# Attention steps of three kinds, with part of the rounding and subtracting moved to GpSimd

## The chip, the cores and the metric

The kernel runs on one core of a Trainium2 chip. A core has TensorE (matrix products, called PE in the profile, with PEld for its weight loads), VectorE (DVE), ScalarE (ACT), GpSimd (POOL) and SyncE (SP, which here only issues DMAs). The metric is the device time of one execution in microseconds, lower is better.

## What is computed

An attention with queries averaged in pairs, followed by a feed-forward block with a squared relu. All arrays are float32.

```
batch, n_heads, seq, head_dim = 4, 8, 1152, 64
q_pool = q.reshape(B, H, S // 2, 2, D).mean(axis=3)
scores = (1 / sqrt(D)) * matmul(q_pool, k^T)
scores = scores - max(scores, axis=-1)
attn   = exp(scores) / (sum(exp(scores)) + 1e-9)
x      = matmul(attn, v), heads side by side: 2304 x 512
h = x @ w_in (512 x 2048); g = s * relu(h)**2 + b; out = g @ w_out (2048 x 512)
```

## The kernel before

**Two formats.** A float32 value is split in a rounded part in a short format of TensorE (names ending in `h` or `vv`) and the rest (`l`); a product of two split values is then three fast products. A product of whole float32 values needs no split but takes TensorE longer: the trace shows it as two matmuls.

**The loop.** 32 heads are taken in 16 pairs. A head has 9 steps, one for each 128 of its keys, so a pair has 18 steps, and n % 18 counts them here ("step 9" is the first step of a pair's second, odd head). Line 600 runs over all 288 steps. A step n issues, on TensorE and in an order written out by hand in `ORD` (line 31):

- the scores of step n (`score_step`, line 466: four matmuls at line 472 into a PSUM tile `s`, of which there are two);
- the value products of step n - 3 (`value_step`, line 491, with `LAG` = 3), into the accumulators `o0`, `o1` of the head, one for each half of the queries;
- one or two products for the maxima of a later pair (`max_unit`, line 426: a matmul at line 442 into `m`, and a maximum by VectorE at line 443).

**Two kinds of steps.** In a split step ScalarE takes the exponential twice, once rounded into `ph` (line 480) and once in place in PSUM (line 482); VectorE subtracts the two into `pl` (line 484); the value products are six matmuls (lines 507, 509, 511: `ph` with `vv`, `ph` with `vl`, `pl` with `vv`, for each half). In a whole step (`WHOLE`, line 33: 7 of 18) ScalarE takes one exponential into `pe` (line 475), and the value products are two float32 products (line 501), which need only `vf`, the values as loaded.

**Around the steps.** `PREP` (line 36) gives the step at which each part of the preparation of the pair after next is issued: `ka`, `kb`, `qt` are transposes by VectorE; `qs` adds the queries on GpSimd; `ha`, `hb`, `qh` round keys and queries on ScalarE (through `hi_of`, line 196); `qm`, `qz` lay out rounded queries on ScalarE; `kl`, `ql` take the rests on GpSimd; `l0`, `l1` (`lay`, line 384) each issue five DMAs on SP. Keys and queries of the pair after that are loaded by 4 and 8 DMAs on SP at step 17 (lines 338, 344). The values of the next head are loaded at step 3 of a head (line 349), rounded and split on GpSimd (`prep_v`, line 412: `vv` and `vl`) at steps 7 and 16 of a pair (`VS`). The maxima of a head are sent by ScalarE's DMA queue (lines 457, 458, tile `c`) at steps 2 and 12. When a head ends, `finish` (line 516) has ScalarE copy four pieces out of `o0` and `o1` (lines 527, 528).

Every engine and every DMA queue works through its instructions in the order of issue. From pair 9 on, weights are also converted, one piece in a pair, with four VectorE and three GpSimd instructions each. After the attention the feed-forward block runs in sweeps over the weights (`Moe`, line 218).

Of the kernel before, what the change touches and what calls it, by code (L numbers as in the profile page):

```python
# [29 lines left out]

ORD = ("svfvvvfvv",) * 8 + ("vvfvvvfvs",)
KB = 384
WHOLE = (1, 3, 6, 9, 11, 13, 16)

PP = (("ka", 0), ("kb", 0), ("ha", 0), ("hb", 1), ("qs", 1), ("qt", 1), ("qm", 2), ("qh", 2), ("qz", 2), ("kl", 2), ("ql", 3), ("l0", 7))
PREP = (("ka", 10), ("qs", 11), ("kb", 13), ("qt", 15), ("ha", 14), ("hb", 14), ("qm", 16), ("kl", 16), ("qh", 16), ("qz", 17), ("ql", 17), ("l0", 0), ("l1", 9))
LD = 1
VS = (7, 16)
XT = (1, 2, 3, 5, 8)
# [15 lines left out]
def attention_moe_kernel(ctx: ExitStack, tc: tile.TileContext, q, k, v, w_in, w_out, s_in, b_in, out):  # L55
# [140 lines left out]
    def hi_of(eng, out, in_):  # L196
        if eng is nc.scalar:
            nc.scalar.activation(out, in_, AF.Copy)  # L198
        else:
            eng.tensor_scalar(out=out, in0=in_, scalar1=1.0, scalar2=0.0, op0=ALU.mult, op1=ALU.add)  # L200
# [150 lines left out]
    def prep_pair(p):  # L351

        kr, qr = kraw.pop(p), qraw.pop(p)
        kT = ap.tile([P, S], F32, tag="kT", bufs=2, name=f"kT{p}")
        qT = ap.tile([P, SQ], F32, tag="qT", bufs=2, name=f"qT{p}")
        qs = ap.tile([P, NBQ, 32], F32, tag="qs", name=f"qs{p}")
        kh = ap.tile([P, S], F32R, tag="kh", bufs=2, name=f"kh{p}")
        qh = ap.tile([P, SQ], F32R, tag="qh", bufs=2, name=f"qh{p}")
        krv = kr.rearrange("p j i -> p (j i)")
        lo, hi = slice(0, SQ), slice(SQ, S)  # L360

        def corner():
            assert holds.get("qm", -1) == p - 1
            for h in range(2):
                d = slice(h * D, (h + 1) * D)
                hi_of(nc.scalar, qm[d, d], qT[d, NT4 * P:])
            holds["qm"] = p

        def k_hi(part, last):
            hi_of(nc.scalar, kh[:, part], kT[:, part])  # L370
            if last:
                khs[p] = kh

        def q_hi():
            hi_of(nc.scalar, qh, qT)
            qhs[p] = qh

        def q_blocks():

            for h in range(2):  # L380
                r = slice(h * D, (h + 1) * D)
                hi_of(nc.scalar, qzs[p % 2][r, h].rearrange("p (t m) -> p t m", t=NT4), qT[r, :NT4 * P].rearrange("p (m t) -> p t m", t=NT4))

        def lay(h):
            hd = 2 * p + h
            kk, qq = kks[hd % 3], qqs[hd % 3].rearrange("p i a n -> p i (a n)")
            r = slice(h * D, (h + 1) * D)
            ks = ((f32(kk[D:P, 0, :]), kT[r]), (f32(kk[0:D]), f32(kh[r]).unsqueeze(1).to_broadcast([D, 2, S])))
            for dst, src in ks[::-1] if hd == 0 else ks:
                nc.sync.dma_start(dst, src)  # L390
            nc.sync.dma_start(f32(qq[0:D, 0, :]), f32(qh[r]))
            nc.sync.dma_start(f32(qq[D:P, 0, :]), f32(qh[r]))
            nc.sync.dma_start(f32(qq[0:D, 1, :]), qT[r])
            holds["k", hd % 3] = hd

        return {
            "ka": lambda: nc.vector.transpose(out=kT[:, lo], in_=krv[:, lo]),
            "qs": lambda: (nc.vector if p < 2 else nc.gpsimd).tensor_tensor(out=qs, in0=qr[:, :, 0, :], in1=qr[:, :, 1, :], op=ALU.add),
            "kb": lambda: nc.vector.transpose(out=kT[:, hi], in_=krv[:, hi]),
            "ha": lambda: k_hi(lo, False),  # L400
            "qt": lambda: nc.vector.transpose(out=qT, in_=qs.rearrange("p j i -> p (j i)")),
            "hb": lambda: k_hi(hi, True),
            "qh": q_hi,
            "qz": q_blocks,
            "kl": lambda: (nc.vector if p == 0 else nc.gpsimd).tensor_tensor(out=kT, in0=kT, in1=f32(kh), op=ALU.subtract),
            "ql": lambda: nc.gpsimd.tensor_tensor(out=qT, in0=qT, in1=f32(qh), op=ALU.subtract),
            "qm": corner,
            "l0": lambda: lay(0),
            "l1": lambda: lay(1),
        }  # L410
# [52 lines left out]
    prob = {}  # L463
    fresh = []

    def score_step(hd, j, eng):
        assert holds["k", hd % 3] == holds["c", hd % 3] == hd
        kk, qq = kks[hd % 3], qqs[hd % 3]
        ps = ps_s.tile([P, 2, 512], F32, tag="s", name=f"s{hd}_{j}")
        for a in range(2):  # L470
            for i in range(2):
                nc.tensor.matmul(ps[:, a, :HALF], kk[:, i, j * P:(j + 1) * P], qq[:, i, a], start=(i == 0), stop=(i == 1))  # L472
        if eng is None:
            pe = late.tile([P, 2, HALF], F32, tag="pe", bufs=PE, name=f"pe{hd}_{j}")
            nc.scalar.activation(pe, ps[:, :, :HALF], AF.Exp, scale=SCALE)
            prob[hd, j] = pe, None
            return
        ph = late.tile([P, 2, HALF], F32R, tag="ph", bufs=PB, name=f"ph{hd}_{j}")
        pl = late.tile([P, 2, HALF], F32R, tag="pl", bufs=PB, name=f"pl{hd}_{j}")
        nc.scalar.activation(ph, ps[:, :, :HALF], AF.Exp, scale=SCALE)  # L480

        nc.scalar.activation(ps[:, :, :HALF], ps[:, :, :HALF], AF.Exp, scale=SCALE)  # L482
        prob[hd, j] = ph, pl
        fresh.append(lambda: eng.tensor_tensor(out=pl, in0=ps[:, :, :HALF], in1=f32(ph), op=ALU.subtract))  # L484

    acc = {}
    xu = {}
# [3 lines left out]
    def value_step(hd, j):  # L491
        assert holds["v", hd % 2] == hd
        vv, vl = vvs[hd % 2], vls[hd % 2]
        ph, pl = prob.pop((hd, j))
        if j == 0:
            acc[hd] = [ps_o.tile([P, 512], F32, tag=f"o{a}", name=f"o{hd}_{a}") for a in range(2)]
        first, last = j == 0, j == NJ - 1
        for a in range(2):
            o = acc[hd][a]
            if pl is None:  # L500
                nc.tensor.matmul(o[:, :HALF], vfs[hd % 2][:, j], ph[:, a], start=first, stop=last)  # L501
                if a == 1 and last:
                    finish(hd)
                for _ in range(3):
                    yield
                continue
            nc.tensor.matmul(o[:, :HALF], vv[:, j], ph[:, a], start=first, stop=False)  # L507
            yield
            nc.tensor.matmul(o[0:D, :HALF], vl[:, j], ph[:, a], start=False, stop=False)  # L509
            yield  # L510
            nc.tensor.matmul(o[:, :HALF], vv[:, j], pl[:, a], start=False, stop=last)  # L511
            if a == 1 and last:
                finish(hd)
            yield

    def finish(hd):
        o = acc.pop(hd)
        p, h = divmod(hd, 2)
        if h == 0:
            xu[p] = (  # L520
                ep.tile([P, 2, HALF], F32, tag="xu", name=f"xu{p}"),
                ep.tile([P, 2, HALF], F32, tag="l", name=f"l{p}"),
            )
        x, l = xu[p]
        r = slice(h * D, (h + 1) * D)
        for a in range(2):
            nc.scalar.activation(x[r, a], o[a][0:D, :HALF], AF.Copy)
            nc.scalar.activation(l[r, a], o[a][D:P, :HALF], AF.Copy, bias=EPS)

        def invert():  # L530
            lt = ep.tile([P, NBQ, 32], F32, tag="lt", name=f"lt{p}")
            nc.vector.transpose(out=lt, in_=l.rearrange("p a n -> p (a n)"))
            inv[p] = lt

        def reciprocal():
            lt = inv[p]
            rc = inv[p] = ep.tile([P, NBQ, 1], F32, tag="rc", name=f"rc{p}")
            nc.vector.reciprocal(rc, lt[:, :, 0:1])

        def spread():  # L540
            rc = inv[p]
            inv[p] = ep.tile([P, NBQ, 32], F32, tag="lt", name=f"rr{p}")
            nc.vector.transpose(out=inv[p], in_=rc.to_broadcast([P, NBQ, 32]))

        def scale():
            xo = xs[p] = ep.tile([P, SQ], F32, tag="xo", name=f"xo{p}")
            nc.gpsimd.tensor_tensor(out=xo, in0=x.rearrange("p a n -> p (a n)"), in1=inv.pop(p).rearrange("p j c -> p (j c)"), op=ALU.mult)

        def send():
            nc.sync.dma_start(xd[hd // H][(hd % H) // 2], xs.pop(p))  # L550

        if h == 1:
            for at, fn in zip(XT, (invert, reciprocal, spread, scale, send)):
                later(at, fn)
# [45 lines left out]
    for n in range(NS + LAG):  # L600
# [4 lines left out]
        units = iter(range((n + AHEAD) * NU // 18, (n + AHEAD + 1) * NU // 18) if n + AHEAD < NS else ())  # L605
        for part in ORD[at] if at is not None else "sff":
            if part == "s" and n < NS:
                score_step(hd, j, None if n % 18 in WHOLE else nc.vector)
            elif part == "f":
                for u in units:  # L610
                    max_unit(u, ps_m, "m")
# [112 lines left out]
```

## Time and profile before

| | us |
|---|---|
| median of 3 runs (lowest to highest) | 1018.68 (1016.87 to 1018.93) |
| the profiled execution, its own time | 1018.46 |
| its span in the profile | 1016.6 |
| busy: PE, PEld | 927.6, 818.0 |
| busy: DVE, ACT, POOL | 651.7, 686.6, 379.6 |

The span is cut by eye into the start (to about 35 us), the attention (to 572 us) and the feed-forward block. A matmul's time in the profile runs from its start to a modelled end, and successive matmuls overlap; what one costs is read from start to start. In the lists, "[1.01 <-DVE pm L443]" is idle time of the engine just before an instruction, and what ended it. Line numbers are those of the kernel before.

### The profile page before, as it was taken

What the parts mean: (1) busy time and instruction counts of PE and PEld (TensorE: products, weight loads), DVE (VectorE), ACT (ScalarE), POOL (GpSimd) and SP (SyncE); (2) the same over time, 40 slices, a digit from 0 to 9 for tenths busy, and PEclk for the clock granted to TensorE, in tenths of its full rate; (3) what the DMA queues carried; (4) which work ended last, traced back from release to release, by engine and by line L of the source; (5) the groups of instructions that cost most, each with busy time, mean ns of one, the idle gap of its engine ahead of it and who ended that gap; (6) DMA issues with size and microseconds to landing.
All of it is one profiled execution on the core that took longest, in us unless ns stands there. A gap on an engine that the chain in (4) does not pass through costs nothing.

```text
span 1016.6 us, 16051 instructions
## 1 busy us (share of the span) xinstructions
PE 927.6 (91%) x5680; PEld 818.0 (80%) x5680; DVE 651.7 (64%) x1191; ACT 686.6 (68%) x1278; POOL 379.6 (37%) x270
## 2 busy tenths in 40 slices
PE   4899999999999999989989987888889999999998
PEld 2778888888788878878878876767779999999997
DVE  5677777777778777877876378777783333333333
ACT  2577677767776787778777777876666555555553
POOL 5323223423342335235523288786772010011000
PEclk9999999999999999999999999999999999999999
DMA  8769765876587669766762245554442313213211
GB/s 166 137 117 190 152 124 108 179 158 126 114 165 161 122 136 184 167 125 136 175 154 55 74 148 186 185 187 145 141 149 84 125 63 114 73 63 92 96 43 42
DMA packets 255311, 131.15 MB, mean 129 GB/s; under 512 B 203776, under 2 KB 227328, under 8 KB 255232
## 3 DMA queue, kind: packets, MB, share of 16 engines
q1 hardware_dynamic: 248064, 130.06, 53.5%
q10 hardware_dynamic: 7168, 0.08, 0.4%
q8 instruction: 45, 0.74, 0.3%
q14 instruction: 34, 0.28, 0.1%
HBM read 68.68 MB, written 18.87 MB: 86 GB/s over the span
## 4 chain that ended last, share of the span: by engine, by line
PE 56%; DVE 20%; ACT 12%; issue 5%; DMA 2%; POOL 2%; ACTq 1%; SPq 0%; DVEq 0%; POOLq 0%
PE y L287 13%; PE h L258 12%; PE s L472 10%; PE o L501 7%; PE m L442 6%; DVE pl L484 4%; DVE pm L443 3%; PE o L511 3%; PE o L509 3%; ACT s L482 3%; ACT ph L480 3%; PE o L507 2%; DVE wAo L152 2%; DVE wAi L152 2%; DVE wabo L151 1%
## 5 line engine op out<-in xcount | busy, mean ns | idle before, releaser
L443 DVE TENSOR_REDUCE pm<-m 128x1 f32<-128x384 f32 x432 | 230.1, 548 | 51.1 <-PE m L442 44.0
L472 PE MATMUL s<-qq,kk 128*128 128x288 f32 x1152 | 208.0, 307 | 18.1 <-DVE pl L484 16.0
L258 PE MATMUL h<-x,wih 128*128 128x256 f32 x1152 | 213.3, 282 | 3.7 <-POOL x L239 3.7
L472 PEld LDWEIGHTS s<-qq,kk 128*128 128x128 f32 x1152 | 170.8, 190 | 40.9 <-DVE pl L484 16.6
L258 PEld LDWEIGHTS h<-x,wih 128*128 128x128 f32 x1152 | 186.9, 189 | 16.6 <-POOL x L239 5.5
L484 DVE TENSOR_TENSOR pl<-s,ph 128x576 fp32r<-128x576 f32 x176 | 132.5, 753 | 85.9 <-ACT s L482 85.8
L442 PE MATMUL m<-kh,qz 128*128 128x384 f32 x384 | 167.5, 446 | 21.5 <-DVE pm L443 21.0
L267 DVE SCALAR_TENSOR_TENSOR t<-h,r 128x256 f32<-128x256 f32 x144 | 60.7, 421 | 168.3 <-ACT r L277 168.3
L480 ACT ACTIVATE ph<-s 128x576 fp32r<-128x576 f32 x176 | 113.9, 647 | 79.6 <-PE s L472 78.6
L258 PE MATMUL h<-x,wil 128*128 128x256 f32 x576 | 162.2, 282 | 0.0
L239 POOL TENSOR_TENSOR x<-xr,x 128x1024 fp32r<-128x1024 f32 x27 | 66.0, 2444 | 229.6 <-ACT x L198 229.6
L501 PE MATMUL o<-pe,vf 128*128 128x288 f32 x448 | 144.7, 407 | 0.0
L287 PE MATMUL y<-woh,gl 128*128 128x512 f32 x288 | 115.7, 402 | 24.9 <-DVE gl L274 24.9
L270 ACT ACTIVATE gh<-t,sb 128x256 fp32r<-128x256 f32 x144 | 86.2, 598 | 65.9 <-DVE t L267 65.8
L482 ACT ACTIVATE s<-s 128x576 f32<-128x576 f32 x176 | 114.2, 649 | 0.0
L287 PE MATMUL y<-wol,gh 128*128 128x512 f32 x288 | 113.2, 393 | 0.0
L287 PE MATMUL y<-woh,gh 128*128 128x512 f32 x288 | 112.8, 392 | 0.0
L258 PEld LDWEIGHTS h<-x,wil 128*128 128x128 f32 x576 | 109.5, 190 | 0.0
L442 PEld LDWEIGHTS m<-kh,qz 128*128 128x128 f32 x384 | 74.7, 195 | 43.1 <-DVE pm L443 33.9
L507 PE MATMUL o<-ph,vv 128*128 128x288 f32 x352 | 107.4, 305 | 0.2 <-POOL vv L200 0.2
L509 PE MATMUL o<-ph,vl 128*64 128x288 f32 x352 | 104.5, 297 | 0.9 <-POOL vl L417 0.9
L511 PE MATMUL o<-pl,vv 128*128 128x288 f32 x352 | 103.6, 294 | 0.0
(73 smaller groups left out, 1481.9 us busy)
## 6 DMA issues: line engine op xcount, KB each, us to landing
kk<-kh SPq DMA_DIRECT2D x32, 576.0 KB, 5.7
kraw<-in_k_dram SPq DMA_DIRECT2D x64, 144.0 KB, 3.1
qraw<-in_q_dram SPq DMA_DIRECT2D x128, 72.0 KB, 2.5
vf<-in_v_dram SPq DMA_DIRECT2D x32, 288.0 KB, 4.4
kk<-kT SPq DMA_DIRECT2D x32, 288.0 KB, 3.3
qq<-qh SPq DMA_DIRECT2D x64, 144.0 KB, 5.6
xr<-xd SPq DMA_DIRECT2D x18, 512.0 KB, 4.0
wsti<-in_moe_w_in_dram SPq DMA_DIRECT2D x16, 512.0 KB, 4.8
```

What stands on the lines that cost most here:

```text
L258: nc.tensor.matmul(h[:, :TB], st[:, c, :], mv[:, c, :], start=(n == 0), stop=(n == 3 * NC - 1))
L287: nc.tensor.matmul(y[:, :DM], st[:, ts_], mv, start=(first and n == 0), stop=(last and n == 2))
L442: nc.tensor.matmul(ps[:, :KB], st, khs[p][:, e * KB:(e + 1) * KB], start=True, stop=True)
L443: nc.vector.tensor_reduce(out=pms[p][:, col, e:e + 1], in_=ps[:, :KB], axis=AX.X, op=ALU.max)
L472: nc.tensor.matmul(ps[:, a, :HALF], kk[:, i, j * P:(j + 1) * P], qq[:, i, a], start=(i == 0), stop=(i == 1))
L480: nc.scalar.activation(ph, ps[:, :, :HALF], AF.Exp, scale=SCALE)
L482: nc.scalar.activation(ps[:, :, :HALF], ps[:, :, :HALF], AF.Exp, scale=SCALE)
L484: fresh.append(lambda: eng.tensor_tensor(out=pl, in0=ps[:, :, :HALF], in1=f32(ph), op=ALU.subtract))
L501: nc.tensor.matmul(o[:, :HALF], vfs[hd % 2][:, j], ph[:, a], start=first, stop=last)
L507: nc.tensor.matmul(o[:, :HALF], vv[:, j], ph[:, a], start=first, stop=False)
L509: nc.tensor.matmul(o[0:D, :HALF], vl[:, j], ph[:, a], start=False, stop=False)
L511: nc.tensor.matmul(o[:, :HALF], vv[:, j], pl[:, a], start=False, stop=last)
```

## The change

- Steps get one of three kinds by their place among the 18 (`KIND`): 7 are `v`, split steps as before, subtracted by VectorE in PSUM (0, 2, 5, 8, 10, 12, 15); 5 are `g` (3, 6, 9, 13, 16), in which ScalarE writes the second exponential into an SBUF tile `pe` and GpSimd subtracts; 6 are `w`, whole (1, 4, 7, 11, 14, 17). Before there were 11, none and 7.
- From the third pair on, keys and queries are rounded by GpSimd and not by ScalarE.
- The two accumulators become one tile of two banks, and `finish` copies two pieces of double width in place of four.
- The parts of the preparation are issued at other steps: `kb` 13 to 12, `ha` 14 to 12, `hb` 14 to 13, `qt` 15 to 14, `kl` 16 to 14, `qm` 16 to 15, `qz` 17 to 16, `l0` 0 to 3; `ka`, `qs`, `qh`, `ql`, `l1` stay.

```diff
-WHOLE = (1, 3, 6, 9, 11, 13, 16)
+KIND = "vwvgwvgwvgvwvgwvgw"
-PREP = (("ka", 10), ("qs", 11), ("kb", 13), ("qt", 15), ("ha", 14), ("hb", 14), ("qm", 16), ("kl", 16), ("qh", 16), ("qz", 17), ("ql", 17), ("l0", 0), ("l1", 9))
+PREP = (("ka", 10), ("qs", 11), ("kb", 12), ("ha", 12), ("hb", 13), ("qt", 14), ("kl", 14), ("qm", 15), ("qh", 16), ("qz", 16), ("ql", 17), ("l0", 3), ("l1", 9))
...
         def k_hi(part, last):
-            hi_of(nc.scalar, kh[:, part], kT[:, part])
+            hi_of(nc.scalar if p < 2 else nc.gpsimd, kh[:, part], kT[:, part])
...
         def q_hi():
-            hi_of(nc.scalar, qh, qT)
+            hi_of(nc.scalar if p < 2 else nc.gpsimd, qh, qT)
...
-    def score_step(hd, j, eng):
+    def score_step(hd, j, kind):
...
-        if eng is None:
+        if kind != "v":
             pe = late.tile([P, 2, HALF], F32, tag="pe", bufs=PE, name=f"pe{hd}_{j}")
+        if kind == "w":
             nc.scalar.activation(pe, ps[:, :, :HALF], AF.Exp, scale=SCALE)
...
-        nc.scalar.activation(ps[:, :, :HALF], ps[:, :, :HALF], AF.Exp, scale=SCALE)
+        full = ps[:, :, :HALF] if kind == "v" else pe
+        nc.scalar.activation(full, ps[:, :, :HALF], AF.Exp, scale=SCALE)
         prob[hd, j] = ph, pl
-        fresh.append(lambda: eng.tensor_tensor(out=pl, in0=ps[:, :, :HALF], in1=f32(ph), op=ALU.subtract))
+        eng = nc.vector if kind == "v" else nc.gpsimd
+        fresh.append(lambda: eng.tensor_tensor(out=pl, in0=full, in1=f32(ph), op=ALU.subtract))
...
-            acc[hd] = [ps_o.tile([P, 512], F32, tag=f"o{a}", name=f"o{hd}_{a}") for a in range(2)]
+            acc[hd] = ps_o.tile([P, 2, 512], F32, tag="o", name=f"o{hd}")
...
-            o = acc[hd][a]
+            o = acc[hd][:, a]
...
-        for a in range(2):
-            nc.scalar.activation(x[r, a], o[a][0:D, :HALF], AF.Copy)
-            nc.scalar.activation(l[r, a], o[a][D:P, :HALF], AF.Copy, bias=EPS)
+        nc.scalar.activation(x[r], o[0:D, :, :HALF], AF.Copy)
+        nc.scalar.activation(l[r], o[D:P, :, :HALF], AF.Copy, bias=EPS)
...
-                score_step(hd, j, None if n % 18 in WHOLE else nc.vector)
+                score_step(hd, j, KIND[n % 18])
```

## Rows read from the trace of the kernel before

**Rows 1.** The page's first part: busy us, share of span, instructions.
```profile
PE 927.6 (91%) x5680; PEld 818.0 (80%) x5680; DVE 651.7 (64%) x1191; ACT 686.6 (68%) x1278; POOL 379.6 (37%) x270
```
**Rows 2.** Stretches: length, busy PE, PEld, DVE, ACT, POOL, granted clock, DMA.
```profile
273.44:290.09 16.65, 15.73 (x103) 14.41 (x101) 13.04 (x23) 10.78 (x20) 2.56 (x3) 1.00 0.82 170
290.09:307.06 16.97, 15.59 (x94) 13.44 (x94) 12.43 (x23) 14.06 (x26) 8.47 (x6) 1.00 0.61 115
...
478.04:513.26 35.22, 31.84 (x195) 27.74 (x194) 28.08 (x50) 26.42 (x48) 14.92 (x11) 1.00 0.74 162
```
**Rows 3.** Groups by line: busy us, mean ns, idle before and its releaser.
```profile
L484 DVE TENSOR_TENSOR pl<-s,ph 128x576 fp32r<-128x576 f32 x176 | 132.5, 753 | 85.9 <-ACT s L482 85.8
L482 ACT ACTIVATE s<-s 128x576 f32<-128x576 f32 x176 | 114.2, 649 | 0.0
...
L417 POOL TENSOR_TENSOR vl<-vf,vv 128x576 fp32r<-128x576 f32 x32 | 45.8, 1432 | 2.3
...
L198 ACT ACTIVATE qz<-qT 64x512 fp32r<-64x512 f32 x32 | 35.7, 1117 | 0.2
...
L527 ACT ACTIVATE xu<-o 64x288 f32<-64x288 f32 x64 | 25.8, 404 | 20.1 <-PE o L511 19.3
...
L200 POOL TENSOR_SCALAR vv<-vf 128x576 fp32r<-128x576 f32 x32 | 21.5, 673 | 96.7 <-DMA vf<-in_v_dram 51.0 <-PE m L442 16.7 <-PE o L511 14.8
...
L198 ACT ACTIVATE kh<-kT 128x576 fp32r<-128x576 f32 x32 | 20.3, 679 | 7.1 <-DVE kT L397 6.8
```
**Rows 4.** TensorE in order of time (start, us, line, matmul): a split and a whole step.
```profile
278.28 0.34 PE L442 MATMUL m<-kh,qz 128*128 128x384 f32 x1
278.45 0.30 PE L509 MATMUL o<-ph,vl 128*64 128x288 f32 x1
278.59 0.29 PE L511 MATMUL o<-pl,vv 128*128 128x288 f32 x1
...
284.81 0.65 PE L501 MATMUL o<-pe,vf 128*128 128x288 f32 x2
...
285.47 0.65 PE L501 MATMUL o<-pe,vf 128*128 128x288 f32 x2
```
**Rows 5.** TensorE in order of time: the two longest stops of a pair.
```profile
275.66 0.80 PE L472 MATMUL s<-qq,kk 128*128 128x288 f32 x4 [0.92 <-DVE pl L484]
...
305.77 0.44 PE L442 MATMUL m<-kh,qz 128*128 128x384 f32 x1 [1.01 <-DVE pm L443]
```
**Rows 6.** One pair's way from `c` to the odd head's first value product, by engine.
```profile
273.44 0.49 ACTq L457 DMA_DIRECT2D qq<-c  x1
...
282.56 0.57 SPq L349 DMA_DIRECT2D vf<-in_v_dram  x1
...
288.86 0.67 POOL L200 TENSOR_SCALAR vv<-vf 128x576 fp32r<-128x576 f32 x1 [7.59 <-PE o L511]
...
290.99 1.43 POOL L398 TENSOR_TENSOR qs<-qraw 128x576 f32<-128x576 f32 x1
...
289.66 0.65 PE L501 MATMUL o<-pe,vf 128*128 128x288 f32 x2
```
**Rows 7.** The same `c` and `vv` in the first and last of 12 pairs.
```profile
105.28 0.49 ACTq L457 DMA_DIRECT2D qq<-c  x1
...
120.34 0.68 POOL L200 TENSOR_SCALAR vv<-vf 128x576 fp32r<-128x576 f32 x1 [7.23 <-PE o L511]
...
478.04 0.49 ACTq L457 DMA_DIRECT2D qq<-c  x1
...
491.09 0.67 POOL L200 TENSOR_SCALAR vv<-vf 128x576 fp32r<-128x576 f32 x1 [5.24 <-PE m L442]
```
**Rows 8.** SP's own waits from 60 to 560 us: total, times, longest.
```profile
SPq L344 <- DMA qq<-c: 103.4, 14, 10.4
```
**Rows 9.** Line 151's durations (ns: min/median/max), 370 to 560 and 580 to 760 us.
```profile
L151 DVE TENSOR_SCALAR wabi<-whmi x3: 428/428/428, 385.3 to 524.1; 128x512 int32<-128x512 int32 x3
...
L151 DVE TENSOR_SCALAR wabi<-whmi x13: 426/1330/1341, 580.1 to 748.4; 128x512 int32<-128x512 int32 x13
```

## The prediction, made before the changed kernel ran

> **What bounds the kernel now.** I read the page's shares first, then stretches of the length of a pair, then TensorE in order of time, then what feeds it. TensorE is busy 91% of the span, its weight loads 80%, no other engine over 68% [rows 1], at a granted clock of 1.00 in every stretch that I read [rows 2]. Only the attention changes, so it is read by itself. A pair takes 33.62 us in the middle of it (the first two rows together) [rows 2]; of 12 pairs from 105.28 to 513.26 us the first eight take 33.6 to 33.8, the last four, with weights to convert, 34.2 to 35.2 (the longest stands in the group) [rows 2].
>
> Busy matmuls overlap, so I count from start to start. A fast product costs 0.13 to 0.14, a maximum's product 0.17 [rows 4]. A whole half-step starts 0.66 before the next, with one maximum's product in between: 0.49 [rows 4]. A pair then needs 18 x 4 x 0.1325 for scores (9.5), 27 x 0.17 for maxima (4.6), 11 x 6 x 0.1325 for split steps (8.7) and 7 x 0.97 for whole ones (6.8): 29.6 of 33.6 us. The other 4 us are the small change at switches and stops. The two longest have an idle time of 0.92, where the scores wait for VectorE's subtraction to give PSUM back, and 1.01, where a maximum's product waits for VectorE's reduction, which stands in VectorE's order behind a subtraction that waits for ScalarE [rows 5]. ScalarE is late there because it has just laid out queries (2 x 1.12) and rounded them [rows 3]. So TensorE bounds the pair, and behind it the order of ScalarE and VectorE: the place where this change works.
>
> **The chain beside it.** One thing runs beside the pairs and matters here. Each pair, SP stops in the loads of queries until the DMA that ScalarE sends for the maxima of the odd head has landed: 14 stops, 103.4 us [rows 8]. Only then come the remaining query loads, the five DMAs of `l0` and the load of the odd head's values, issued at 282.56 where `c` was sent at 273.44; `vv` starts on GpSimd at 288.86, and `vl` ends as the next instruction starts, 290.99 [rows 6]. From `c` to `vv` it is 15.06 in the first and 13.05 in the last of 12 pairs [rows 7], 14.07 on average, at most 15.42. Before, this had just room: the first value step of the odd head (step 9) is whole, needs `vf` alone and starts at 289.66 [rows 6].
>
> **The change, part by part, for one pair.**
>
> *Kinds of steps.* TensorE: one whole step (0.97) becomes a split one (6 x 0.1325 = 0.80), 0.17 saved, on its path. VectorE: 4 subtractions fewer, 4 x 0.75 = 3.0 [rows 3]. ScalarE: one exponential more, 0.65 [rows 3]. GpSimd: 5 subtractions of 128x576 float32; the trace has the operation at 1.43 (`vl`) [rows 3], both inputs in SBUF, so 7.2. The PSUM tile of a `g` step is free after ScalarE's second exponential, 0.75 before it would be with VectorE behind.
>
> *Rounding.* ScalarE loses three instructions of 0.68, 2.0; GpSimd does the same shape in 0.67 (`vv`) [rows 3], 2.0. GpSimd goes from 11.03 of 33.62 us (2.56 and 8.47) [rows 2] to about 20, and from 14.92 to about 24 of 35 with weights. It has room on average; what counts is its order.
>
> *The held subtraction.* Step 9 is now `g`. In GpSimd's order its subtraction stands behind `vv` and `vl` of the odd head (issued at step 7), which wait for the load. Its exponentials are there at about 286, but it starts when `vl` ends: 14.07 + 0.75 + 1.38 after `c`, and ends 1.42 later, 17.6 after `c`. The value products of step 9 need it as their third matmul, which stood at 290.09, 16.65 after `c`. So TensorE waits about 1 us there if nothing ahead of it gets faster, and more by whatever it gains ahead. Queued behind: `qs`, then roundings of keys, the subtraction of step 13 and `kl`; step 13's result is used three steps later, so 5.6 us of queue fit. This chain sets the first part of the pair. The keys are transposed one step earlier, so one query load more may have gone before SP stops: 0 to 0.5 off the chain; I take 0.3, thus 17.3.
>
> *The second part*, from 290.09 to the next `c` at 307.06, is 16.97 [rows 2]. The whole step that went lies here (values of steps 9 to 17 held four, now three): 0.17 off. Stops, summed from start to start, are about 2.2, of which 1.2 is the one at 305.77 [rows 5]. ScalarE has 2.0 less rounding, the layout of queries a step earlier, VectorE half its subtractions. The bounds for what goes are 0.3 (only the small ones) and 2.2 (all); nearest to the long one is ScalarE's work just ahead of it, which is what the change removes, so I take 1.5: 15.3. What is late next is the product itself. Pair: 17.3 + 15.3 = 32.6, 1.0 less.
>
> *The accumulators.* Four copies of 0.40 become two of double width, by the exponentials' rows 0.65 each: 0.3 less a head [rows 3]. But the copies now start when the second half is done, and the next head's first product waits for both: 0 to 0.5 late, twice a pair. At the odd head the held subtraction hides it, at the even head it falls in the first part, where TensorE will wait anyway. So nothing; with that cover gone 16 x 1.0 = 16 us.
>
> *The moved parts.* `l0` issues five DMAs on SP at step 3 and no longer at 0; they stay ahead of the load of values and behind the query loads, at whose stop they already wait until step 4. Nothing, and 0 to 0.5 a pair if SP's order of waits shifts. `kb`, `ha`, `hb`, `qt`, `kl` come earlier by one or two steps and are needed at step 3 of the next pair: nothing. `ql` ends GpSimd's list of the pair, by my count at about step 2, before SP's stop ends.
>
> *Weights.* VectorE's line 151 takes 428 ns in the attention and 1330 in the later stretch where GpSimd is busier [rows 9]. Four such instructions in six pieces, each 0.9 longer, would be 22 us of VectorE; in the attention it has slack, and three of the four come while GpSimd waits for the load. I take 1 us, between 0 and 22. The Trainium skill (SBUF — State Buffer, Who interferes with whom) says that VectorE in a two-port mode, or with two SBUF inputs, and GpSimd shut each other out for a whole instruction. By that rule more GpSimd work lengthens these, and leaves the subtraction from PSUM alone; the rows agree as far as they go.
>
> **The sum.** 12 pairs x 1.0 = 12. The last 1.75 pairs (from 513 to 572 us) have no loads and so no chain; there the stops count whole, 1.7 of 3.3 plus 0.17: 3.3. For the first two pairs I take nothing. Less 1 for the weights: 14.3. From the profiled execution's 1018.46 (span 1016.6 and 1.9 around it, 0.2 under the median): 1004.
>
> **Rivals.**
> - *TensorE alone sets the pair.* If the loads come early enough (SP no longer stops for `c`, or one step later in the order), the held subtraction is in time and the pair is 29.5 plus about 1.5, 31: 2.6 x 13.5 = 35 us less, 984. For it: idle SP time of 7 to 10 us a pair [rows 8]; against: nothing in the change takes that wait away.
> - *The held subtraction takes more than the stops give back: slower.* Same place. It decides when `c` to subtraction exceeds 33.62 - 15.3 = 18.3, 1.0 beyond my value; three of the 12 pairs have a `vv` that late (over 15 after `c`). With 18.3 and only 0.7 of the stops saved the pair is 34.4, 0.8 x 12 = 10 us longer, less 3 at the end: 1025. For it: the wait is new in every pair, and the stops' cause on ScalarE gets an exponential back; against: the long stop sits right behind the work that leaves ScalarE.
> - *VectorE shut out during the weights.* The 22 us in full undo the gain: 1025. Against: VectorE's slack.
> - *No change.* The two cancel, within 0.2% (2 us, about what a measurement of this kernel can tell from none): 1018.
>
> **How the numbers follow.** Forecast (993 to 1013) 0.50; TensorE alone (975 to 993) 0.15; subtraction wins 0.20; VectorE shut out 0.04; cancel 0.11. Faster 0.65, same 0.11, slower 0.24. The range runs from 983, half of the first rival, to 1025, the middle of the second.
>
> **What would show it.** Right: matmuls of line 511 with `pl` of step 9 idle 1 to 3 us each pair, released by GpSimd's subtraction; 17 to 18 us from `c` to the end of that subtraction; no stop over 0.5 before the next `c`; VectorE 3 us and ScalarE 2 us less a pair. Wrong: no such wait (then 984), or waits for GpSimd also at steps 13 and 16, or the stop at the end of the odd head still there (then 1018 or above).

## The result and the profile after

The change made the kernel slower: 1023.93 us (1022.44 to 1026.02, four runs) against 1018.47 (1016.87 to 1018.93), a ratio of 1.0058 with a 95% interval of 1.0036 to 1.0079. I had forecast 1004. The profiled execution took 1022.44, its span 1020.6, 4.0 over that of before.

The load did move. This is the page's first part of the kernel after, to be held against [rows 1]:

```profile
PE 919.3 (90%) x5712; PEld 819.4 (80%) x5712; DVE 618.8 (61%) x1127; ACT 663.6 (65%) x1188; POOL 519.9 (51%) x392
```

TensorE has 8 us less work, VectorE 33, ScalarE 23; GpSimd has 140 more. So the time has gone into waiting. The groups by line name the wait (busy us, mean ns, idle before and its releaser, as in [rows 3]):

```profile
L474 PE MATMUL s<-qq,kk 128*128 128x288 f32 x1152 | 213.2, 310 | 35.9 <-ACT pe L478 20.8 <-DVE pl L489 12.3 <-POOL vv L202 1.2
...
L489 POOL TENSOR_TENSOR pl<-pe,ph 128x576 fp32r<-128x576 f32 x80 | 114.3, 1428 | 159.5 <-ACT pe L486 159.5
...
L489 DVE TENSOR_TENSOR pl<-s,ph 128x576 fp32r<-128x576 f32 x112 | 84.4, 754 | 49.0 <-PE o L516 21.7 <-ACT s L486 20.9 <-PE s L474 3.7
...
L531 ACT ACTIVATE xu<-o 64x576 f32<-64x576 f32 x32 | 20.6, 644 | 41.5 <-PE o L506 22.9 <-PE o L516 16.3 <-POOL vl L419 1.2
```

The scores' matmuls (L474) sit idle 20.8 us for `pe` of L478, the single exponential of a *whole* step. Before, no such wait was among the long ones, as the same group shows there:

```profile
L472 PE MATMUL s<-qq,kk 128*128 128x288 f32 x1152 | 208.0, 307 | 18.1 <-DVE pl L484 16.0 <-POOL vv L200 1.3 <-DVE pm L443 0.2
```

In order of time, all engines, one steady pair (its odd head's `c` goes at 276.50):

```profile
291.38 0.68 POOL L202 TENSOR_SCALAR vv<-vf 128x576 fp32r<-128x576 f32 x1 [4.19 <-DMA vf<-in_v_dram]
...
291.74 0.70 PE L474 MATMUL s<-qq,kk 128*128 128x288 f32 x4
...
292.00 0.65 ACT L531 ACTIVATE xu<-o 64x576 f32<-64x576 f32 x1 [1.17 <-PE o L516]
292.66 0.65 ACT L532 ACTIVATE l<-o 64x576 f32<-64x576 f32 x1
293.33 0.65 ACT L478 ACTIVATE pe<-s 128x576 f32<-128x576 f32 x1
...
293.50 1.41 POOL L489 TENSOR_TENSOR pl<-pe,ph 128x576 fp32r<-128x576 f32 x1
...
294.03 0.80 PE L474 MATMUL s<-qq,kk 128*128 128x288 f32 x4 [1.59 <-ACT pe L478]
...
295.11 0.29 PE L516 MATMUL o<-pl,vv 128*128 128x288 f32 x1
```

Read it from the bottom. The scores of step 12 start at 294.03, after a stop of 1.59. They wait for `pe` of step 11, which ends at 293.98. That exponential stands in ScalarE's order behind the two copies of the even head's accumulator, and these wait for the last value product. TensorE's written order puts the scores of steps 11 (291.74) and 12 back to back at the change of heads, with nothing between. In the built program the two have the same PSUM tile: the pool gave step 12 not the tile of step 10 but that of step 11. The trace bears it out: the scores of step 12 wait for ScalarE's semaphore in 13 pairs, and all 13 have this stop; with the tile of step 10, a `v` step, they would wait for VectorE's. (Step 10 has the tile of step 9 in five pairs, without a stop over 0.28.) In the kernel before, neighbours share a tile too, at steps 2, 7, 10 and 17 (and 14 in one pair), but never at 3 or 12, where two scores stand back to back.

The stretches, odd `c` to odd `c`, with the steady pair cut where the values of step 9 take their `pl` (length, busy PE, PEld, DVE, ACT, POOL, granted clock, DMA), against [rows 2]:

```profile
276.50:295.11 18.61, 16.00 (x102) 14.38 (x101) 11.70 (x21) 12.08 (x21) 7.85 (x7) 1.00 0.83 172
295.11:309.87 14.76, 14.74 (x97) 13.48 (x95) 11.21 (x21) 11.12 (x19) 12.05 (x10) 1.00 0.57 107
...
70.04:109.38 39.34, 33.45 (x197) 30.17 (x195) 23.15 (x42) 23.19 (x39) 23.31 (x19) 0.91 0.80 151
...
480.49:515.22 34.73, 31.10 (x197) 27.87 (x195) 26.24 (x46) 24.73 (x42) 23.78 (x20) 1.00 0.72 152
515.22:549.75 34.53, 30.85 (x197) 27.89 (x195) 25.00 (x43) 23.13 (x39) 21.10 (x16) 1.00 0.44 106
```

From these points the 4.0 us, and the 18.3 by which the forecast missed, can be laid out (us; the last column is what the prediction's sum gave):

| stretch | before | after | difference | forecast |
|---|---|---|---|---|
| start, to the third odd `c` | 105.28 | 109.38 | +4.1 | 0 |
| eight pairs without weights | 269.25 | 267.21 | -2.0 | -8.0 |
| four pairs with weights | 138.73 | 138.63 | -0.1 | -3.0 |
| the rest of the span | 503.34 | 505.38 | +2.0 | -3.3 |

### The profile page after: what moved, and what is told of

Its sections match the earlier page's. It is cut to its first block, busy times and chain, and to the rows that moved or that the text cites. A ratio compares the mean times of both kernels' runs of the same rounds, so it can differ in the third digit from the quotient of the medians.

```text
span 1020.6 us, 16183 instructions
## 1 busy us (share of the span) xinstructions
PE 919.3 (90%) x5712; PEld 819.4 (80%) x5712; DVE 618.8 (61%) x1127; ACT 663.6 (65%) x1188; POOL 519.9 (51%) x392
## 4 chain that ended last, share of the span: by engine, by line
PE 66%; DVE 14%; ACT 7%; issue 4%; POOL 3%; DMA 2%; SPq 1%; DVEq 0%; ACTq 0%; POOLq 0%
PE s L474 13%; PE y L289 13%; PE h L260 12%; PE o L506 8%; PE m L444 7%; PE o L512 5%; PE o L516 4%; PE o L514 4%; DVE wAo L154 2%; DVE wAi L154 2%; DVE wabi L153 1%; DVE wabo L153 1%; DVE whmi L151 1%; DVE whmo L151 1%; ACT h L273 1%
## 5 line engine op out<-in xcount | busy, mean ns | idle before, releaser
L474 PE MATMUL s<-qq,kk 128*128 128x288 f32 x1152 | 213.2, 310 | 35.9 <-ACT pe L478 20.8
L474 PEld LDWEIGHTS s<-qq,kk 128*128 128x128 f32 x1152 | 172.9, 191 | 54.8 <-ACT pe L478 26.2
L489 POOL TENSOR_TENSOR pl<-pe,ph 128x576 fp32r<-128x576 f32 x80 | 114.3, 1428 | 159.5 <-ACT pe L486 159.5
L483 ACT ACTIVATE ph<-s 128x576 fp32r<-128x576 f32 x192 | 124.9, 651 | 106.4 <-PE s L474 80.4
L444 PE MATMUL m<-kh,qz 128*128 128x384 f32 x384 | 158.7, 423 | 8.3 <-DVE pm L445 7.8
L506 PE MATMUL o<-pe,vf 128*128 128x288 f32 x384 | 124.5, 408 | 0.0
L512 PE MATMUL o<-ph,vv 128*128 128x288 f32 x384 | 115.4, 301 | 7.1 <-issue 3.6
L514 PE MATMUL o<-ph,vl 128*64 128x288 f32 x384 | 114.0, 297 | 0.9 <-POOL vl L419 0.9
L489 DVE TENSOR_TENSOR pl<-s,ph 128x576 fp32r<-128x576 f32 x112 | 84.4, 754 | 49.0 <-PE o L516 21.7
L516 PE MATMUL o<-pl,vv 128*128 128x288 f32 x384 | 113.6, 296 | 0.0
L279 ACT ACTIVATE r<-h 128x256 f32<-128x256 f32 x144 | 54.5, 378 | 59.4 <-PE h L260 58.6
```

Source lines behind the costliest of these rows:

```text
L444: nc.tensor.matmul(ps[:, :KB], st, khs[p][:, e * KB:(e + 1) * KB], start=True, stop=True)
L489: fresh.append(lambda: eng.tensor_tensor(out=pl, in0=full, in1=f32(ph), op=ALU.subtract))
```

## The experiments

Theory 1: the tile shared at step 12 costs most of the pairs' gain. Theory 2: the start loses by a load of values that goes late. Theory 3: VectorE is shut out by GpSimd where weights are converted. The rival to all three was the prediction's own chain, with its held subtraction. Numbers are medians; each run was timed beside the kernel before (1017.7 to 1018.0).

**1. Score tiles in strict turn.** The kernel after, and

```diff
-    ps_s = ... tile_pool(name="ps_s", bufs=2, space=PSUM)
+    ps_s = ... tile_pool(name="ps_s", bufs=1, space=PSUM)
...
-        ps = ps_s.tile([P, 2, 512], F32, tag="s", ...)
+        ps = ps_s.tile([P, 2, 512], F32, tag=f"s{(hd * NJ + j) % 2}", ...)
...
-            max_unit(u, *((ps_m, "m") if u % 2 == 0 else (ps_s, "s")))
+            max_unit(u, *((ps_m, "m") if u % 2 == 0 else (ps_s, f"s{u // 2 % 2}")))
```

The last pair of lines does the same for the maxima ahead of the first step, which use the same tiles.

> The kernel after, with one thing changed: the two PSUM tiles of the scores are given to the steps in strict turn, so that step 12 no longer gets the tile of step 11. Theory 1 (the forecast's chain is not what binds; the scores of step 12 wait for the tile of step 11, which ScalarE empties only after the value step of step 8 and the two copies of the even head's accumulator): the stop of 1.6 us at step 12 goes in each of some 14 pairs; the next limits (the held subtraction, which ended 17.4 after c against 18.6 for the part that it bounds, and the accumulators' copies) are about 1.2 us behind, so the steady pair goes from 33.37 to about 32.2 us and the time from 1023.9 to about 1007. Rival, the one of the prediction (the held subtraction and the load of values set the pair): the pair stays at 33.3 to 33.5 and the time within 1021 to 1026, the stop only moves to the products with the lower part of step 9.

Measured: 1010.71, ratio 0.9936 (0.9919 to 0.9952), 13.2 less than after. The steady pair is 32.2 in four of eight and at most 33.52. The same place, all engines (`c` at 302.70):

```profile
317.58 1.43 POOL L489 TENSOR_TENSOR pl<-pe,ph 128x576 fp32r<-128x576 f32 x1
...
317.93 1.37 PE L474 MATMUL s<-qq,kk 128*128 128x288 f32 x8
...
318.85 0.65 ACT L532 ACTIVATE l<-o 64x576 f32<-64x576 f32 x1
...
319.60 0.37 PE L512 MATMUL o<-ph,vv 128*128 128x288 f32 x1 [0.30 <-issue]
...
320.11 0.30 PE L516 MATMUL o<-pl,vv 128*128 128x288 f32 x1
```

Both steps' scores now run as one (x8), and ScalarE's copies no longer stand in their way. TensorE then starts the odd head 0.1 us behind the second copy: the copies are what is late next. Theory 1 holds, some 4 us short of its number. The Trainium skill (Perfetto Trace Analysis, Matmuls) says that independent groups of matmuls should take PSUM banks in rotation, so that emptying one overlaps the next group. These rows agree at one of the two places of a pair where two groups of scores are neighbours in TensorE's order; experiments 5 and 11 show what the rule is worth elsewhere here.

**2. Two accumulators, four copies,** as before the change.

```diff
-            acc[hd] = ps_o.tile([P, 2, 512], F32, tag="o", name=f"o{hd}")
+            acc[hd] = [ps_o.tile([P, 512], F32, tag=f"o{a}", name=f"o{hd}_{a}") for a in range(2)]
...
-        nc.scalar.activation(x[r], o[0:D, :, :HALF], AF.Copy)
-        nc.scalar.activation(l[r], o[D:P, :, :HALF], AF.Copy, bias=EPS)
+        for a in range(2):
+            nc.scalar.activation(x[r, a], o[a][0:D, :HALF], AF.Copy)
+            nc.scalar.activation(l[r, a], o[a][D:P, :HALF], AF.Copy, bias=EPS)
```

> The kernel after with the accumulators as they were before: two tiles and four copies of single width. Theory 1 (copies of double width, which can start only when the second half is done, push back ScalarE's exponential for step 11 and with it the scores of step 12): the first two of four copies run beside the second half's products, the stop at step 12 falls from 1.6 to about 0.8 us, a pair from 33.37 to about 32.6, the time from 1023.9 to about 1012. Rival (the held subtraction sets the first part of the pair; copies are hidden there, as the prediction said): 1021 to 1026, pair 33.3 to 33.5.

Measured: 1020.16, ratio 1.0017 (1.0003 to 1.0031), 3.8 less than after. The steady pair is 33.05: 0.3 gained where 0.8 was expected. The direction is the theory's, the size is under half, and the way is another: the stop at step 12 stays at 1.55 to 1.57. It comes 17.2 after `c` and not 17.5: the 0.3 is won ahead of it, at the copies of the odd head's accumulators, where the next head's first value product starts 0.07 after `c` and not 0.43.

**3. The load of values ahead of `l1`,** once, at the start: `prep1.pop("l1")()` moves from step 9 to step 12, behind `load_v`.

> The kernel after, with the five DMAs that lay out the second head of the second pair (l1, step 9 there) issued behind the load of values of step 12 in place of ahead of it, once, at the start. Theory 2 (the start loses 4 us because SP's stop for c holds that value load until 68.0 us, and TensorE, after idle times of 3.35 and 0.92 at 73.6 us, runs at a granted clock of 0.50 to 0.55 until about 81): the idle times and the stretch at half clock go, 1023.9 becomes about 1019 to 1020, all of the difference lying before 109 us. Rival (the start is slower because ScalarE and GpSimd work in another order at 30 to 40 us): the odd head's maxima are still sent 4 us later than before at 109 us and the time stays at 1023 to 1025.

Measured: 1026.28, ratio 1.0080 (1.0063 to 1.0097): no gain. The third odd `c` did come 2.2 earlier (107.16), and TensorE's stop of 3.35 at 73 us was gone; but the pair from 173.96 took 35.84, and 2.5 went back there, so that the profiled execution, the fastest of six, took 1022.59 against 1022.44 after. Half of theory 2.

**4. Weights early.** `STA = (0, 4, 6, 9, 11, 13)` becomes `(0, 1, 3, 9, 11, 13)`.

> The kernel after, with the steps at which a piece of weights is converted in the attention changed from 0, 4, 6, 9, 11, 13 to 0, 1, 3, 9, 11, 13: VectorE's four instructions stand where GpSimd has less to do. Theory 3 (VectorE is shut out by GpSimd in these: line 151 takes 1545 ns in five of six pieces, 417 to 428 before, and a product for the maxima then waits 1.0 to 2.4 us for VectorE): the instructions take 0.4 to 0.7 us, the pairs with weights go from 34.6 towards 33.4, at 5 pairs 4 to 6 us: about 1018 to 1020. Rival (the pairs with weights were as long before, 34.2 to 35.2, when line 151 took 428 ns, so something else makes them long): they stay at 34.3 to 34.8 and the time at 1022 to 1025.

Measured: 1020.32, ratio 1.0025 (1.0015 to 1.0036), 3.6 less than after. The first of VectorE's instructions on a piece, in the three of six pieces that the traces call `whmi`, 370 to 560 us (count, ns: min/median/max, first and last start). Before:

```profile
L149 DVE TENSOR_SCALAR whmi<-whmi x3: 417/417/417, 384.8 to 523.5; 128x512 f32<-128x512 f32 x3
```

After:

```profile
L151 DVE TENSOR_SCALAR whmi<-whmi x3: 1545/1545/1546, 386.0 to 524.7; 128x512 f32<-128x512 f32 x3
```

Experiment 4:

```profile
L151 DVE TENSOR_SCALAR whmi<-whmi x3: 383/384/385, 382.4 to 519.9; 128x512 f32<-128x512 f32 x3
```

So VectorE is shut out: the same instruction takes 1545 ns beside an instruction of GpSimd, and 417 or 384 where GpSimd has none (what sets these two apart stays open). One piece in the trace of after, in order of time:

```profile
524.50 1.43 POOL L551 TENSOR_TENSOR xo<-xu,rr 128x576 f32<-128x576 f32 x1
524.66 1.55 DVE L151 TENSOR_SCALAR whmi<-whmi 128x512 f32<-128x512 f32 x1
...
529.34 0.44 PE L444 MATMUL m<-kh,qz 128*128 128x384 f32 x1 [2.37 <-DVE pm L445]
```

L151 starts while GpSimd works and ends 0.28 after that GpSimd instruction does. The Trainium skill (SBUF — State Buffer, Who interferes with whom) has the rule: whoever issues first holds the shared ports for its whole instruction. These rows agree. It costs less than I thought: the pairs with weights fell by 0.1 to 0.5 only (to 34.36 to 34.41), because another stop of 0.57 to 0.63 for a maximum came up 8 us after `c`, where VectorE's instructions on weights now stand ahead of the reduction; the pair from 515 us, where the stop of 2.37 stood, fell from 34.53 to 33.00. Theory 3 for the last pair, its rival for the others.

Nor did the shutting out end: it moved to the fourth instruction, L157. After, and in experiment 4:

```profile
L157 DVE TENSOR_SCALAR wabi<-wAi x3: 411/420/1394, 390.7 to 530.8; 128x512 int32<-128x512 int32 x3
...
L157 DVE TENSOR_SCALAR wabi<-wAi x3: 1598/1610/1666, 386.0 to 523.5; 128x512 int32<-128x512 int32 x3
```

With the other three pieces it takes over 1.2 us twice in six after, five times in six here, and yet no stop of TensorE over 0.28 hangs on it. The gain came from where VectorE is held, not from holding it less.

**5. The kernel before, score tiles in strict turn** (the same edit as in 1).

> The kernel before, with nothing changed but that the two PSUM tiles of the scores are given to the steps in strict turn. Theory 1 (the tile that step 12 shares with step 11 was a loss that came with the new order of kinds; the trace of before has no stop of the scores for ScalarE's single exponential): no gain to speak of, 1013 to 1022, steady pair 33.3 to 33.8, and the change in strict turn against before in strict turn is worth some 7 to 12 us. Rival (strict turn is a gain of its own that has nothing to do with the change, before could have had it too): the pair falls to about 32.4 and the time to about 1003 to 1008.

Measured: 1022.69, ratio 1.0047 (1.0032 to 1.0062): slower. Strict turn is no gain of its own. Before, the shared tiles at steps 2, 7, 10 and 17 were harmless or better, by 4.9 us in all (1017.74 beside it). With the tiles in turn on both sides the change is worth 1022.69 - 1010.71 = 12.0 us.

**6. Experiments 1 and 4 together.**

> Experiments 1 and 4 together: strict turn of the score tiles and the weights' steps 0, 1, 3, 9, 11, 13. The pairs with weights were 33.6 to 33.7 in experiment 1 and the one before the last 34.89; experiment 4 took 0.1 to 0.5 from each of the former and 1.5 from the latter against the kernel after. If the two add up: 1010.7 - 1 - 2.5, about 1007, the last full pair 32.2 to 33.0. Rival (with TensorE ahead by 1.2 us a pair the earlier VectorE instructions meet the stop at step 2 to 4, which was 0.63 in experiment 4): 1009 to 1012, last pair 34 or more.

Measured: 1007.28, ratio 0.9898 (0.9883 to 0.9913), as the sum said. The pairs with weights are 33.25 but for the first (33.78), the last full pair 33.09.

**7. Strict turn, step 9 whole again,** step 11 subtracted by GpSimd: `KIND = "vwvgwvgwvwvgvgwvgw"`.

> Strict turn of the score tiles, and the kinds of steps 9 and 11 exchanged: step 9 whole as it was before, step 11 subtracted by GpSimd, so that GpSimd's subtraction behind the load of the odd head's values is needed two steps later. The prediction's chain (c, load of values, vv, vl, subtraction of step 9, third product of step 9) binds, after experiment 1, only in the two pairs of 33.2 and 33.5 us from 171 to 238 us, where the products wait 1.0 us for GpSimd. If that is right these two pairs fall to about 32.2 to 32.5 and the others stay: 1010.7 - 2, about 1008 to 1009. Rival (the chain binds in every pair and strict turn only uncovered it): all pairs fall below 32, time about 1003 or less.

Measured: 1013.95, ratio 0.9960 (0.9947 to 0.9973), 3.2 more than experiment 1. The two pairs did fall, from 33.22 and 33.52 to 32.51 and 32.49: they were the held subtraction's. But the other pairs rose by 0.3, and those with weights by 1.1 (34.8). So the chain binds in a few pairs only, and step 9 whole isn't the better order.

**8. Strict turn, ScalarE rounds again** (`hi_of(nc.scalar, ...)` in `k_hi` and `q_hi`).

> Strict turn of the score tiles, with keys and queries rounded by ScalarE again, at the new steps of the preparation. The prediction's second part (the stop of 1.01 us for a maximum ahead of the odd head's c is there because ScalarE is late after laying out and rounding queries): the stop comes back with 0.5 to 1.0, the steady pair goes from 32.2 to about 32.9, the time from 1010.7 to about 1019. Rival (four subtractions fewer on VectorE and the layout one step earlier are enough): no stop over 0.5 there, the pair stays at 32.2 to 32.4, the time 1009 to 1012.

Measured: 1015.34, ratio 0.9983 (0.9966 to 0.9999), 4.6 more than experiment 1, though its third odd `c` goes 2.0 earlier (104.69); the steady pair is 32.67. The size was about right, the place not. The stop for a maximum ahead of `c` did not come back. A stop of the scores of step 1 came up instead, 0.46 to 0.61 in 14 pairs, here in TensorE's order of time:

```profile
266.76 0.79 PE L474 MATMUL s<-qq,kk 128*128 128x288 f32 x4 [0.58 <-ACT pe L478]
```

**9. Experiment 6 with two accumulators.**

> Experiment 6 (strict turn, weights early) with the accumulators as they were before: two tiles, four copies of single width. In experiment 1 the first product of the next head starts 0.1 us behind the end of the second copy and after 0.30 us of idle time, at both heads. Theory (the prediction's nothing for the accumulators is wrong, they cost 0 to 0.5 a head): a pair falls from 32.2 to 31.6 to 31.9, the time from 1007.3 to about 1000 to 1003. Rival (the copies are no longer late with the score tiles in turn; experiment 2 gained 0.3 a pair only by way of the stop at step 12): 1006 to 1009, pair 32.1 to 32.3.

Measured: 1000.83, ratio 0.9834 (0.9817 to 0.9850): better than both kernels by far more than the intervals. The accumulators cost 6.4 us once the shared tile was out of the way. Here the prediction's chain shows at last. Two pairs and a piece of the first, as stretches:

```profile
202.39:237.26 34.87, 32.29 (x197) 29.23 (x196) 22.90 (x42) 23.88 (x43) 19.88 (x16) 0.95 0.69 137
...
301.11:332.91 31.80, 30.53 (x197) 27.84 (x196) 22.98 (x42) 23.78 (x43) 19.90 (x16) 1.00 0.74 150
...
219.00:222.00 3.00, 1.41 (x6) 1.10 (x6) 0.56 (x1) 1.62 (x3) 3.00 (x3) 0.85 1.01 222
222.00:225.00 3.00, 3.00 (x15) 2.90 (x15) 2.52 (x5) 0.94 (x2) 0.89 (x2) 0.58 0.26 52
```

TensorE in order of time, the same piece:

```profile
219.59 0.34 PE L514 MATMUL o<-ph,vl 128*64 128x288 f32 x1 [0.57 <-POOL vl L419]
...
220.95 0.48 PE L516 MATMUL o<-pl,vv 128*128 128x288 f32 x1 [1.02 <-POOL pl L489]
```

In that pair `vv` starts 14.97 after `c`, `vl` and the held subtraction follow, and TensorE waits 1.6 us in all; the clock's fall to 0.58 adds to it (experiment 12 has the same pair without that fall).

**10. Experiment 6 with the early load of values of experiment 3.**

> Experiment 6 with the load of values at the start ahead of the five DMAs of l1, as in experiment 3. There 2.2 us were won before 107 us and lost again by one pair of 35.84 (a stop of 1.59 at step 12, one of 0.73 for GpSimd right behind it, and a granted clock of 0.95). Theory (the late load of values is the start's loss, and the later loss needed the stop at step 12): the maxima of the odd head leave at 105 to 106 instead of 108.5 us, no pair after it over 33.5 outside the weights, the time about 1004 to 1005. Rival (moving the five DMAs only hands the wait on to the next loads): 1007 to 1009.

Measured: 1009.74, ratio 0.9917 (0.9894 to 0.9940): the rival. The third odd `c` goes at 108.62, and the pair from 173.03 takes 35.29. Delaying `l1` only hands the wait on.

**11. Experiment 1 with tiles shared at steps 8 and 15** (with steps 7 and 14, whole as 11 is).

```diff
+        ps = ps_s.tile(..., tag=f"s{(hd * NJ + j + (8 <= (hd * NJ + j) % 18 < 15)) % 2}", ...)
```

> Experiment 1 with a tile shared by neighbours at two other steps: step 8 gets the tile of step 7, step 15 that of step 14 (7 and 14 are whole, as 11 is), in every pair; the rest in turn. Theory 1 in its narrow form (sharing is dear at step 12 because TensorE's order puts the scores of steps 11 and 12 back to back there and the copies of the accumulator stand in ScalarE's order between; elsewhere other products stand between the scores of neighbours): no stop at 8 or 15 over 0.5, pair 32.2 to 32.6, time 1009 to 1016. Rival (any sharing by neighbours costs a stop of about 1.6 us): two stops a pair, pair 34 or more, time over 1030.

Measured: 1019.10, ratio 1.0011 (0.9998 to 1.0024), 8.4 more than experiment 1. The steady pair is 32.6 in four of eight, 0.4 over that of experiment 1 for *two* shared tiles, without a stop over 0.4 at the shared steps; the others take 32.8 to 34.2, one with a stop of 0.92 for `pe` at step 15, one of the two shared steps, two with one of 0.8 to 1.0 for the held subtraction. So in most pairs a shared tile costs little where other products stand between, though more than the 1009 to 1016 that I gave it, and far less than the rival's 1030.

**12. Experiment 9 with the third pair rounded by ScalarE** (`p < 3`).

> Experiment 9 with keys and queries of the third pair too rounded by ScalarE (GpSimd begins with the fourth). Theory (the start is slower because, with GpSimd rounding the third pair, SP stops for the first odd head's c one DMA earlier and the load of values behind it goes at 67.5 to 68.0 in place of 65.1 to 65.2 us, as it did in experiment 8 where ScalarE rounds): that load is issued at about 65, TensorE's stop at 73 us falls from 3.6 to about 1, the granted clock stays at 1.00 and the stretch from the second to the third odd head's c goes from 36.9 to about 35; the time from 1000.8 to about 999. Rival (SP's place is set by something else in experiment 8, such as its other roundings): the load at 67 to 68, the stretch 36.5 to 38.5, the time 1000 to 1003.

Measured: 1001.15, ratio 0.9841 (0.9825 to 0.9858), the same as experiment 9. The load of values goes at 67.71, the stretch to the third odd `c` is 37.11: the rival. Where GpSimd begins to round doesn't set the start. The pair that took 34.87 in experiment 9 is of use here: its stops are nearly the same (0.48 and 1.01 at 219.6 and 220.9 us), the granted clock stays at 1.00, and it takes 33.26.

```profile
202.54:235.80 33.26, 30.79 (x197) 27.77 (x196) 22.91 (x42) 23.79 (x42) 19.91 (x16) 1.00 0.72 144
219.00:222.00 3.00, 1.50 (x10) 1.17 (x10) 0.89 (x2) 1.71 (x3) 3.00 (x3) 1.00 1.01 228
222.00:225.00 3.00, 3.00 (x21) 2.69 (x20) 2.48 (x6) 1.29 (x3) 0.91 (x3) 1.00 0.32 60
```

So some 1.5 of experiment 9's 34.87 goes with the fall of the clock.

**What stays open at the start.** After, SP and TensorE in order of time:

```profile
57.46 0.62 SPq L392 DMA_DIRECT2D kk<-kh  x1
...
68.01 0.54 SPq L351 DMA_DIRECT2D vf<-in_v_dram  x1
...
73.61 0.41 PE L512 MATMUL o<-ph,vv 128*128 128x288 f32 x1 [3.35 <-POOL vv L202]
```

The same in experiment 8:

```profile
57.71 0.47 SPq L393 DMA_DIRECT2D qq<-qh  x1
...
65.22 0.57 SPq L351 DMA_DIRECT2D vf<-in_v_dram  x1
...
70.83 0.41 PE L512 MATMUL o<-ph,vv 128*128 128x288 f32 x1 [1.07 <-POOL vv L202]
```

The stretch behind that stop in after (the granted clock is the third number from the end):

```profile
76.00:78.00 2.00, 2.00 (x10) 1.86 (x8) 0.00 (x0) 0.38 (x1) 1.79 (x2) 0.50 0.86 136
```

and in experiment 8:

```profile
76.00:78.00 2.00, 2.00 (x17) 1.92 (x16) 1.86 (x4) 1.70 (x4) 0.00 (x0) 1.00 0.96 187
```

SP stops for the `c` sent at 55.5 us (that of the second pair's even head; my expectation took it for the first odd head's) either at `kk<-kh` (after, experiments 1, 9 and 12: the load goes at 67.5 to 68.0) or one DMA later, at `qq<-qh` (before, experiments 7 and 8: 65.1 to 65.5). In every trace the DMAs of both queues have the same eight semaphores for their completion, and the stopped DMA is the next one with the semaphore of `c`: it starts 0.06 to 0.07 after that `c` has landed (in after at 57.40). By order of start `c` is the 56th DMA in after and experiment 1 and the 57th in before and experiments 7 and 8. What shifts that place stays open (not the third pair's rounding, experiment 12). The load is 2.8 us later by it; the granted clock of 0.50, the lower of its two levels (1.2 GHz), behind the stop of 3.35 adds to that. But the early load alone does not save the start. In experiment 7 it goes at 65.46, and yet the stop is 2.38, the granted clock falls, and the stretch to the third odd `c` takes 37.08 (35.14 in experiment 8):

```profile
71.84 0.61 PE L512 MATMUL o<-ph,vv 128*128 128x288 f32 x1 [2.38 <-POOL vv L202]
...
76.00:78.00 2.00, 2.00 (x6) 1.55 (x5) 0.56 (x1) 0.49 (x1) 0.00 (x0) 0.50 0.98 193
```

## Why the prediction was wrong

**The step that failed: "This chain sets the first part of the pair", 17.3.** It was 18.61 in the steady pair, and the chain did not set it. In the eight steady pairs of after the held subtraction ended 16.9 to 18.6 after `c`, 17.7 on average, close to the 17.6 of my working, and TensorE waited for GpSimd's `pl` once in the whole attention, for 0.3 (a weight load):

```profile
L516 PEld LDWEIGHTS o<-pl,vv 128*128 128x128 f32 x384 | 72.8, 190 | 9.6 <-POOL pl L489 0.3
```

It was close behind, though: in three of the eight it ended 0.05 to 0.31 before the product that takes it. What set the first part was the stop of 1.59 at step 12, for a tile of scores. I had costed the score tiles only for how soon a `g` step gives its own back, and took their order of use as unchanged. The new order of kinds changed it. With the tiles in turn (experiment 1) the first part is 17.42 in five pairs, and 17.57 to 18.65 in the three where the chain is later than that.

**The second part** was 14.76, forecast 15.3: nearly all of the stops there went, not 1.5 of 2.2 us. Experiment 8 shows that the stop at 305.77 [rows 5] did not go because rounding left ScalarE, as I had argued, but with the other edits: fewer subtractions or the earlier layout, which no run separates. Rounding was worth 4.6 us, net of the earlier start, by another stop.

**The accumulators: "nothing"** was a mis-sized term: 3.8 us in experiment 2, 6.4 between experiments 6 and 9, of the 16 that I gave as the price without cover. I did name the cover, and where it fails; I trusted it too far, since the held subtraction covers only a few pairs.

**The last pairs: -3.3** came out at +2.0. Experiments 4 and 6 take back 1.5 to 1.8 of it in the last full pair (the stop of 2.37 at 529 us); my 1 us for the weights was placed in the pairs where slack does hide most of it, not in the last one.

**The start: nothing** came out at +4.1. Of that, 2.7 went with the tiles in turn (the third odd `c` of experiment 1 goes at 106.73); the rest stands beside the late load, the stop and the half clock, and what sets those stays open, as above. Of the prediction's "0 to 0.5 a pair if SP's order of waits shifts", the shift was seen, once, and at several times that price.

**What was right.** Per steady pair VectorE lost 2.6 us (forecast 3.0), ScalarE 1.6 (2.0 of rounding and 0.6 of copies less 0.65: 1.95), GpSimd gained 8.9 (9.2). The rival "held subtraction takes more" gave 1025, near the time, but by a mechanism that didn't happen in the kernel after. Of the other rivals only the shutting out of VectorE was seen, and moving it gave back 3.6 us, not 22. With the tiles in turn the change gains 12.0 us (experiments 5 and 1), beside the 14.3 of the forecast; part of that nearness is chance, since the accumulators and the start were missing from the sum.

## What to carry to other kernels

When a change alters how long buffers are held, look up which buffer each step gets in the new order, not only how soon each is free: a pool that gives a step the tile of its neighbour puts a wait between two groups of matmuls that stand back to back. Price the handover at the places where the written order has nothing between. A gain found behind a lost one is still there: here tiles in turn, the first of VectorE's instructions on weights moved away from GpSimd's, and the old accumulators made the slower kernel 1.7% faster than before.

## What the hardware showed that I had not expected

- A VectorE instruction of 0.4 us (417 or 384 ns) took 1545 ns beside GpSimd, in nearly every piece, so the delay is not an average but a whole instruction of GpSimd's.
- Short stops can cost more than their length. Behind stops of 0.57 and 1.02 us (experiment 9, 219 to 221 us) the granted clock was 0.58 from 222 to 225 us; the single stop of 1.59 in the steady pair of after left it at 1.00, and so did stops of 1.07 and 0.90 in experiment 8 (71 to 73 us) and of 0.48 and 1.01 in experiment 12 (219 to 221 us). Which of the two comes was not to be told from the length of the stops.
